# An attention kernel with a soft mixture of experts behind it: two weight tiles loaded into buffers of attention that have gone dead, and the second layer's columns taken in pieces of 128, 256 and 128 with outputs of 256 KB

## The chip, the cores and the metric

The kernel runs on one core of a Trainium2 chip. The metric is device time in microseconds (us), the median of three executions. Five engines work side by side: PE (matrix products, with its own weight loads, PEld), DVE, ACT and POOL (elementwise work and copies), and SP, which here issues nearly all transfers. Sixteen DMA engines move the data between the large memory and the core's buffers.

## The reference

```python
# attention, batch 8, heads 8, sequence 576, head size 64
q_rot, k_rot = rotate(q), rotate(k)                    # rotary embedding
scores = q_rot @ k_rot.T / sqrt(D)
attn = softmax(scores)
x = (attn @ v) -> rows of all heads side by side       # 4608 x 512
# soft mixture of 8 experts with 4 slots each
logits = x @ phi                                       # 4608 x 32
d = softmax over the 4608 rows of logits
slot_input = d.T @ x                                   # 32 slots x 512
for e in range(8):
    h = max(slot_input[e] @ w1[e], 0)                  # 512 -> 1024
    slot_out[e] = h @ w2[e]                            # 1024 -> 512
c = softmax over the 32 slots of logits
out = c @ slot_out                                     # 4608 x 512, float32
```

`w1` and `w2` are 16.8 MB each, the output is 9.4 MB. The slots (32 in all) are so few that the experts are mostly a matter of reading weights.

## The kernel before

**Attention.** 32 pairs of heads (`p` = 0 to 31) go through a fixed list of steps: load and rotate q and k, write them as halves of 16-bit numbers into a tile `hl` (pool `stk`, three buffers of 4,608 bytes a partition, taken in turn), compute row maxima, scores and exponentials, and the products with v (`av`, L363). The order is written out by hand: the tables `WHEN` and `EARLY` give each step a time and the steps are recorded in that order. On PE, ACT and DVE that order is kept to the end of the program; on SP and POOL only up to `steady.close()` (L793), and behind it a scheduler orders POOL's instructions.

**Weights.** The two layers come as 64 tiles of 512 KB (128 partitions of 4 KB), loaded by `load_w` in the order of the list `order`. 28 of them go to the pool `wp` during attention. Near its end `trickle` loads 7 more (pools `wa`, `wx`) where `PACE` says so. The other 29 follow attention, each as soon as a place is free: `wk` and five in `wl` where attention's buffers were (`release_att`), two in `lw` (L800) where the last transposed rows were, two in `wb` (L878) where the normalised rows `xn` were, seven (`N_LEAD`) and then twelve into buffers of `wp` whose first-layer weights have been used by `ffn1` (L892). SP issues all of this from one queue in program order; each transfer also waits for the one eight places ahead of it in the queue.

**Combine weights.** `c_split(q)` (L556) writes the softmax over slots for two batches as a rounded part and a rest into a tile `csp`, the first by ACT, the second by POOL or DVE. `c_tr(q)` transposes it on PE and `c_evac` copies it to `cst` and `crt`. In the kernel before, the tiles `csp0`, `csp1` and two of `cst` are placed in the space of `hl` as soon as the last scores are done (`release_stk`), and `c_split(0)` and `c_split(1)` stand there, with both subtractions on DVE.

**From attention to the experts.** Between L797 and L882 a chain of small steps over PE, DVE, ACT and POOL ends in `slot_t`, the slots' inputs. Two of its links are on POOL: `e_blk` (L857) and `zw` (L859), which PE needs at L863 and L864.

**Experts and output.** `ffn1` has four calls of 16 products of 512 columns (32 in the trace, since each is run in two passes). `ffn2_steps(mh, so)` computes one half of the 512 output columns (256) in 16 steps of four products (eight in the trace), evacuated to `so`. `gather(mh, so)` adds the slots' parts together into `sl`. `combine(mh, sl, b)` makes the output of one batch `b` (or of the rest rows, `b` = 8): two products of 128 columns of `sl` with 512 rows, copied by ACT and by DVE into the halves of one buffer, and one transfer of 512 KB. The two halves are interleaved: `GROUPS` says which combines of the first half stand between how many steps of the second (a negative number is a count of steps).

```python
GROUPS = ((0, 1, -3), (2, 3, -4), (4, 5, 6, -8), (7, "gather", 8))   # L41
```

So PE runs combines 0 and 1, three steps, combines 2 and 3, four steps, 4 to 6, eight steps, then combine 7, the gather of the second half, and combine 8.

Of the kernel before, what the change touches and what calls it, by code (L numbers as in the profile page):

```python
# [19 lines left out]
DM = H * D  # L20
# [10 lines left out]
N_WL = 5  # L31
# [9 lines left out]
GROUPS = ((0, 1, -3), (2, 3, -4), (4, 5, 6, -8), (7, "gather", 8))  # L41
# [13 lines left out]
PACE = {("m_rows", 29): 3, ("m_rows", 30): 3, ("m_rows", 31): 1}  # L55
# [102 lines left out]
def attn_softmoe(ctx, tc, qk, v, phi, w1, w2, cs, ident, sel, seg, out):  # L158
# [5 lines left out]
    wp = ctx.enter_context(tc.tile_pool(name="wp", bufs=N_W))  # L164
    left = ctx.enter_context(ExitStack())
# [5 lines left out]
    early = ctx.enter_context(ExitStack())  # L171
    stk = early.enter_context(tc.tile_pool(name="stk", bufs=N_HL))
# [61 lines left out]
    def high(p, t, c=full):  # L234
        if p not in halves:
            halves[p] = stk.tile([P, 4, S], F16, name="hl")
        nc.scalar.copy(out=halves[p][:, 1 + t, c], in_=loaded[p][:, t, 0, c])  # L237
# [318 lines left out]
    def c_split(q):  # L556
# [3 lines left out]
        (nc.gpsimd if 2 <= q < C_POOL else nc.vector).tensor_tensor(  # L560
# [51 lines left out]
    order.insert(N_W + N_CST + N_WA, swap[-1])  # L612
# [17 lines left out]
    def release_io():  # L630
# [4 lines left out]
        later.extend([(wa, N_CST)] * N_CST + [(wx, N_WA)] * N_WA)  # L635
# [139 lines left out]
    for when, n, q in events:  # L775
# [7 lines left out]
        if (n, q) in scores:  # L783
            scores.remove((n, q))
            if not scores:
# [4 lines left out]
                c_split(1)  # L790
# [5 lines left out]
    next(stat)  # L796
    vals.close()  # L797
# [109 lines left out]
    def ffn2_steps(mh, so):  # L907
        for grp in range(2):
            op = ps_a.tile([P, 512], F32, name="o_ps")
            og = op[:, 0:256]  # L910
            for f in range(8):
                for x in range(4):
                    nc.tensor.matmul(og[32 * x:32 * x + 32, :], lhsT=hts[grp][:, f // 4, f % 4, 32 * x:32 * x + 32],  # L913
                                     rhs=w_tiles[4 * E + 16 * mh + 8 * grp + 4 * (f // 4) + x][:, f % 4, :],
                                     start=(f == 0), stop=(f == 7), tile_position=(0, 32 * x))
                if f == 7:
                    nc.scalar.copy(out=so[:, 0, grp, :], in_=og)
                    nc.vector.tensor_tensor(out=so[:, 1, grp, :], in0=og, in1=so[:, 0, grp, :], op=ALU.subtract)
# [48 lines left out]
    sos = [wp.tile([P, 2, 2, 256], F32R, name="w_exp", bufs=N_W) for _ in range(2)]  # L967
# [10 lines left out]
    steps = ffn2_steps(1, sos[1])  # L978
# [70 lines left out]
```

## Time and profile before

| | us |
|---|---|
| median of 3 runs (492.08 to 494.11) | 492.92 |
| the profiled execution | 490.22 |
| its span, first to last instruction | 488.0 |
| end of attention's last product, from the span's start | 420.9 |
| first-layer products (`ffn1`) begin | 432.3 |
| second-layer products (`ffn2_steps`) begin | 449.1 |
| first output transfer issued | 460.3 |
| the DMA engines fall idle | 486.3 |

| engine | busy us | share of the span |
|---|---|---|
| PE | 458.1 | 94% |
| PEld | 369.2 | 76% |
| DVE | 370.1 | 76% |
| ACT | 298.0 | 61% |
| POOL | 288.0 | 59% |

PE is busy nearly all the time up to 476 us and then not at all, while the DMA engines, half idle during attention, are full from 421 to 486 us. A share over the whole span hides that; the part after attention has to be read by stretches.

### The profile page before, as it was taken

How to read it: one execution, taken by the hardware profiler on the slowest of the kernel's cores; microseconds unless marked ns; L12 is line 12 of the kernel's file. 1: busy time of each engine (PE TensorE's matmuls, PEld its weight loads, DVE VectorE, ACT ScalarE, POOL GpSimd, SP SyncE). 2: the span in 40 equal slices, each digit the busy share in tenths (PEclk: the TensorE clock that was granted, in tenths of full speed). 3: DMA queues.
4: the chain of work that ended last, by engine and by line, in shares of the span. 5: the costliest groups of instructions: out<-in, count | busy, mean ns of one | idle time of the engine just before them, and what ended most of it. 6: DMA issues, size and time to landing. Idle time of an engine off the chain costs nothing.

```text
span 488.0 us, 23673 instructions
## 1 busy us (share of the span) xinstructions
PE 458.1 (94%) x10505; PEld 369.2 (76%) x10505; DVE 370.1 (76%) x624; ACT 298.0 (61%) x681; POOL 288.0 (59%) x318
## 2 busy tenths in 40 slices
PE   4399999999999999999999999999999999999990
PEld 2168788888888888888887888788889888844550
DVE  4979998788879887988898879888977853433271
ACT  2156666775677577657765776567657757463551
POOL 2884869919892879397949694978669102120000
PEclk9689999999999999999999999999999999999996
DMA  7246645563554455435543563254450343499988
GB/s 268 104 184 229 251 136 199 172 222 135 200 170 167 147 195 176 179 126 205 172 174 132 173 205 136 98 167 167 165 189 26 125 160 111 172 375 406 390 352 348
DMA packets 29509, 94.04 MB, mean 193 GB/s; under 512 B 5088, under 2 KB 6880, under 8 KB 29408
## 3 DMA queue, kind: packets, MB, share of 16 engines
q1 hardware_dynamic: 29388, 92.54, 52.2%
q8 instruction: 82, 1.34, 1.1%
q14 instruction: 19, 0.16, 0.1%
q10 hardware_dynamic: 20, 0.00, 0.0%
HBM read 83.02 MB, written 9.44 MB: 189 GB/s over the span
## 4 chain that ended last, share of the span: by engine, by line
PE 87%; DVE 6%; ACT 2%; DMA 2%; issue 1%; SPq 0%; POOL 0%; DVEq 0%; POOLq 0%; ACTq 0%
PE s_ps L363 32%; PE s_ps L328 25%; PE s_ps L275 7%; PE s_ps L343 3%; PE o_ps L913 3%; PE sp_ps L892 3%; PE s_ps L458 2%; DVE nm L277 2%; PE s_ps L717 2%; PE s_ps L437 2%; ACT a_t L329 2%; PE s_ps L284 1%; PE c_ps L939 1%; DVE x_in L232 1%; PE s_ps L520 1%
## 5 line engine op out<-in xcount | busy, mean ns | idle before, releaser
L228 POOL TENSOR_TENSOR x_in<-x_in,cs_sb 128x288 f32<-128x288 f32 x248 | 231.6, 967 | 86.0 <-DMA x_in<-in_qk 77.7
L277 DVE TENSOR_REDUCE nm<-s_ps 128x2 f32<-128x576 f32 x256 | 187.9, 752 | 53.0 <-PE s_ps L275 51.9
L329 ACT ACTIVATE a_t<-s_ps 128x576 f32<-128x576 f32 x256 | 145.7, 659 | 10.3 <-PE s_ps L328 10.2
L363 PEld LDWEIGHTS s_ps<-v_in,a_t 128*64 128x64 f32 x4608 | 138.7, 137 | 11.3 <-ACT a_t L329 3.8
L363 PE MATMUL s_ps<-v_in,a_t 128*64 128x66 f32 x4608 | 144.8, 222 | 0.6 <-ACT a_t L329 0.3
L328 PE MATMUL s_ps<-hl 64*128 64x288 f16 x1536 | 133.8, 283 | 0.3 <-ACT a_t L329 0.2
L328 PEld LDWEIGHTS <-hl 64*128 64x128 f16 x1536 | 79.4, 94 | 19.7 <-issue 9.2
L328 PE MATMUL s_ps<-peak,lift 64*128 64x288 f16 x512 | 75.3, 283 | 0.0
L275 PE MATMUL s_ps<-hl 64*128 64x288 f16 x512 | 66.3, 288 | 6.0 <-DVE nm L277 3.2
L393 ACT COPY o_sb<-s_ps 128x528 f32<-128x528 f32 x31 | 18.6, 600 | 73.6 <-PE s_ps L363 73.6
L411 POOL TENSOR_TENSOR xn<-o_sb,rr 128x640 f32<-128x640 f32 x31 | 43.3, 1404 | 30.8 <-PE s_ps L520 13.9
L237 ACT CAST hl<-x_in 128x576 f16<-128x576 f32 (+1 forms) x66 | 41.0, 657 | 26.0 <-DVE x_in L232 25.9
L241 DVE TENSOR_TENSOR hl<-x_in,hl 128x1152 f16<-128x1152 f32 x32 | 51.7, 1614 | 2.0 <-ACT hl L237 2.0
L232 DVE TENSOR_TENSOR x_in<-x_in 128x1152 f32<-128x1152 f32 (+2 forms) x36 | 50.3, 1399 | 0.1
L275 PEld LDWEIGHTS <-hl 64*128 64x128 f16 x512 | 30.3, 95 | 21.3 <-issue 10.1
L328 PEld LDWEIGHTS <-lift 64*128 64x128 f16 x512 | 27.1, 94 | 4.4
L363 PE MATMUL s_ps<-v_in,a_tr 64*64 64x66 f32 x1152 | 26.1, 224 | 0.0
L363 PEld LDWEIGHTS s_ps<-v_in,a_tr 64*64 64x64 f32 x1152 | 21.6, 133 | 4.9 <-issue 4.2
L286 DVE TENSOR_REDUCE nm<-s_ps 128x2 f32<-128x576 f32 x32 | 23.9, 749 | 1.2 <-PE s_ps L284 0.8
L343 PE MATMUL s_ps<-hl 64*64 64x256 f16 (+1 forms) x384 | 23.5, 287 | 0.1
L347 ACT ACTIVATE a_tr<-s_ps 128x512 f32<-128x512 f32 x32 | 19.1, 597 | 0.8
L447 ACT COPY xt<-s_ps 128x576 f32<-128x576 f32 x31 | 19.0, 656 | 0.0
(168 smaller groups left out, 408.1 us busy)
## 6 DMA issues: line engine op xcount, KB each, us to landing
x_in<-in_qk SPq DMA_DIRECT2D x62, 576.0 KB
w_exp<-in_w SPq DMA_DIRECT2D x63, 512.0 KB
v_in<-in_v SPq DMA_DIRECT2D x32, 330.0 KB
out<-w_exp SPq DMA_DIRECT2D x18, 512.0 KB
peak<-mr SPq DMA_DIRECT2D x126, 0.5 KB
x_in<-in_qk SPq DMA_DIRECT2D x4, 288.0 KB
cs_sb<-in_cs SPq DMA_DIRECT2D x2, 288.0 KB
peak<-mr SPq DMA_DIRECT2D x32, 0.2 KB
```

The lines of the kernel that those rows point to most:

```text
L228: eng.tensor_tensor(out=x[:, :, c], in0=x[:, :, c], in1=cs_sb[:, :, c], op=ALU.mult)
L232: nc.vector.tensor_tensor(out=x[:, t, 0, c], in0=x[:, t, 0, c], in1=x[:, t, 1, c], op=ALU.add)
L237: nc.scalar.copy(out=halves[p][:, 1 + t, c], in_=loaded[p][:, t, 0, c])
L241: nc.vector.tensor_tensor(out=hl[:, 0:4:3], in0=x[:, :, 0], in1=hl[:, 1:3], op=ALU.subtract)
L275: nc.tensor.matmul(s[c, h, 0:HC], lhsT=hl[rows[h], QH, P * j + c.start:P * j + c.stop], rhs=hl[rows[h], KH, half[n]], start=True, stop=True)
L277: nc.vector.tensor_reduce(out=nm[:, n, j:8:4], in_=s[:, :, 0:HC], axis=AX.X, op=ALU.max, negate=True)
L286: nc.vector.tensor_reduce(out=nm[:, :, 8], in_=s[:, :, 0:HC], axis=AX.X, op=ALU.max, negate=True)
L328: nc.tensor.matmul(s[c, h, 0:HC], lhsT=lhs, rhs=rhs, start=(x == 0), stop=(x == 3))
L329: nc.scalar.activation(out=ats[p, b][:, :, half[n]], in_=s[:, :, 0:HC], func=AF.Exp, scale=SCALE)
L343: nc.tensor.matmul(s[rows[h ^ n], n, 0:w] if n else s[rows[h], 0, 512 - w:512], lhsT=lhs, rhs=rhs, start=(x == 0), stop=(x == 3))
L363: nc.tensor.matmul(o[rows[c], h, VW * u:VW * u + VW], lhsT=lhs, rhs=v, start=(i == 0 and u == 0), stop=(left_av[p] == 0 and u == 3 + (c == ...
L411: eng.tensor_tensor(out=xn, in0=t[:, :, :, 0:64], in1=rr.unsqueeze(3).broadcast_to([P, 2, 5, 64]), op=ALU.mult)
```

## The change

1. The pool `stk` stays open to the end. Of its three buffers, two take second-layer weight tiles (`N_WH` = 2), loaded by `trickle` at the end of attention (the `PACE` of the last `m_rows` is 3 instead of 1). These two leave the pool `wl`, which has three places instead of five.
2. The third `hl` buffer takes `csp0` and `crt`. `csp1` and the two `cst` tiles move to attention's released space, so `c_split(1)` moves behind `release_att`, and its subtraction goes to POOL.
3. The second layer's 512 columns are computed in pieces of 128, 256 and 128 (`COLS`) instead of two halves; `w2` is laid out to match. `combine` issues one transfer of 256 KB for each 128 columns, so there are 36 outputs instead of 18; a buffer of 512 KB holds two of them.
4. The interleaving table is used twice: combines of piece 0 among steps of piece 1, combines of piece 1 among steps of piece 2.

```diff
-N_WL = 5
+N_WL = 3
+N_WH = 2
+COLS = ((0, 128), (128, 384), (384, 512))
+W2 = (4 * E, 4 * E + 8, 4 * E + 24)
-GROUPS = ((0, 1, -3), (2, 3, -4), (4, 5, 6, -8), (7, "gather", 8))
+GROUPS = (((0, 1, -3), (2, 3, -4), (4, 5, 6, -8), (7, "gather", 8)), ((0, 1, -3), (2, 3, -4), (4, 5, 6, -8), (7, "gather", 8)))
-PACE = {("m_rows", 29): 3, ("m_rows", 30): 3, ("m_rows", 31): 1}
+PACE = {("m_rows", 29): 3, ("m_rows", 30): 3, ("m_rows", 31): 3}
...
+    stk = ctx.enter_context(tc.tile_pool(name="stk", bufs=N_HL))
     left = ctx.enter_context(ExitStack())
...
-        (nc.gpsimd if 2 <= q < C_POOL else nc.vector).tensor_tensor(
+        (nc.gpsimd if 1 <= q < C_POOL else nc.vector).tensor_tensor(
...
-        if layer == 0:
+        if pool is stk:
+            wt = stk.tile([P, 2 * S], F32, name="hl")[:, 0:1024].rearrange("p (c x) -> p c x", c=4 if layer else 2)
+            pace = None
+        elif layer == 0:
...
-        later.extend([(wa, N_CST)] * N_CST + [(wx, N_WA)] * N_WA)
+        later.extend([(wa, N_CST)] * N_CST + [(wx, N_WA)] * N_WA + [(stk, N_HL)] * N_WH)
...
     def release_stk():
-        early.close()
-        cp = ctx.enter_context(tc.tile_pool(name="cp", bufs=1, side="right", reuse_waits="tile"))
-        csps = [cp.tile([P, 2, 5, 2, NS], F32R, name=f"csp{i}") for i in range(N_CS)]
-        cst = [cp.tile([P, 2, 4, P], F32R, name=f"cst{i}") for i in range(N_CE)]
-        c_tiles.append([cst, None, csps])
+        t = stk.tile([P, 2 * S], F32R, name="hl")
+        first = t[:, 0:640].rearrange("p (b j a n) -> p b j a n", b=2, j=5, a=2)
+        c_tiles.append([[], t[:, 640:2 * S].rearrange("p (b x) -> p b x", b=B), [first]])
...
                 release_stk()
                 c_split(0)
-                c_split(1)
...
     release_att()
     stat = stat_tasks(B - 1)
     next(stat)
+    c_split(1)
     vals.close()
...
-    def combine(mh, sl, b):
-        k = (9 * mh + b) % (N_WA + N_WB)
-        ob = (wb.tile([P, 4, 256], F32, name=f"w_exp{k}") if k < N_WB else
-              extra[0].tile([P, 4, 256], F32, name="w_exp", bufs=N_WA))
-        for jj in range(2):
+    stage = []
+
+    def combine(k, sl, b):
+        first, n = COLS[k][0] // P, (COLS[k][1] - COLS[k][0]) // P
+        for jj in range(n):
+            if not stage:
+                i = next(staged) % (N_WA + N_WB)
+                ob = (wb.tile([P, 2, 512], F32, name=f"w_exp{i}") if i < N_WB else
+                      extra[0].tile([P, 2, 512], F32, name="w_exp", bufs=N_WA))
+                stage.extend((ob[:, 0], ob[:, 1]))
             o = ps_t.tile([P, 512], F32, name="c_ps")
...
-            ob2 = ob.rearrange("p j m -> p (j m)")
-            (nc.vector.tensor_copy if jj else nc.scalar.copy)(out=ob2[:, 512 * jj:512 * jj + 512], in_=o)
-        nc.sync.dma_start(out=out[mh, b], in_=ob2)
+            ob = stage.pop(0)
+            (nc.scalar.copy if len(stage) else nc.vector.tensor_copy)(out=ob, in_=o)
+            nc.sync.dma_start(out=out[first + jj, b], in_=ob)
```

What moves on SP, at the end of attention and behind it (`hl` is a tile of attention that now takes weights, `wk` and `w_exp` are weight tiles, `peak_106` belongs to attention's last pair). Before:

```order
L313 DMA peak_106<-mr 2x2x32
L626 DMA w_exp<-in_w 128x1024
L626 DMA wk<-in_w 128x1024
L626 DMA w_exp<-in_w 128x1024 x5
L660 DMA seg_in<-in_seg 128x320
L626 DMA w_exp<-in_w 128x1024 x2
L626 DMA w_exp_9997<-in_w 128x1024
L626 DMA w_exp_9999<-in_w 128x1024
L626 DMA w_exp<-in_w 128x1024 x19
```

and of the changed kernel:

```order
L315 DMA peak_106<-mr 2x2x32
L631 DMA w_exp<-in_w 128x1024
L631 DMA hl<-in_w 128x1024 x2
L631 DMA wk<-in_w 128x1024
L631 DMA w_exp<-in_w 128x1024 x3
L664 DMA seg_in<-in_seg 128x320
L631 DMA w_exp<-in_w 128x1024 x2
L631 DMA w_exp_9992<-in_w 128x1024
L631 DMA w_exp_9994<-in_w 128x1024
L631 DMA w_exp<-in_w 128x1024 x19
```

Two transfers stand ahead of `wk` and two fewer behind it; the rest of the weights keep their order.

What moves on POOL, between attention and the first layer (`zacc`, `zs`, `zw` are the sums over rows, `e_blk` a factor for the slots, `seg_sb` a table for the gather). Before:

```order
L497 TENSOR_SCALAR zacc<-zacc,al 128x2
L498 TENSOR_TENSOR zacc<-zacc,sd 128x2
L854 TENSOR_SCALAR zs<-zacc 128x1
L855 TENSOR_TENSOR zs<-zs,zacc 128x1
L857 TENSOR_TENSOR e_blk<-id_sb,e_sel 128x128
L859 TENSOR_SCALAR zw<-e_sel,zs 128x32
L560 TENSOR_TENSOR csp_9611<-cn_sb,csp_9611 128x10x32
L661 CAST seg_sb<-seg_in 128x320
L560 TENSOR_TENSOR csp_9612<-cn_sb,csp_9612 128x10x32
```

and of the changed kernel:

```order
L499 TENSOR_SCALAR zacc<-zacc,al 128x2
L500 TENSOR_TENSOR zacc<-zacc,sd 128x2
L858 TENSOR_SCALAR zs<-zacc 128x1
L859 TENSOR_TENSOR zs<-zs,zacc 128x1
L562 TENSOR_TENSOR csp_9836<-cn_sb,csp_9836 128x10x32
L665 CAST seg_sb<-seg_in 128x320
L861 TENSOR_TENSOR e_blk<-id_sb,e_sel 128x128
L863 TENSOR_SCALAR zw<-e_sel,zs 128x32
L562 TENSOR_TENSOR hl<-cn_sb,hl 128x10x32
L562 TENSOR_TENSOR csp_9836<-cn_sb,csp_9836 128x10x32
```

The subtraction of `c_split(1)` and the copy of `seg_sb` now stand ahead of `e_blk` and `zw`.

## Rows read from the trace of the kernel before

**Rows 1.** Page: shares of the last-ending chain by engine; output transfers.
```profile
PE 87%; DVE 6%; ACT 2%; DMA 2%; issue 1%; SPq 0%; POOL 0%; DVEq 0%; POOLq 0%; ACTq 0%
...
out<-w_exp SPq DMA_DIRECT2D x18, 512.0 KB
```

**Rows 2.** Windows: engines' busy us (count), granted clock, DMA share, GB/s.
```profile
411.00:420.00 9.00, 9.00 (x232) 7.80 (x223) 1.88 (x7) 6.65 (x15) 2.94 (x3) 1.00 0.17 58
420.00:421.00 1.00, 1.00 (x48) 0.86 (x44) 0.01 (x1) 0.00 (x0) 0.00 (x0) 1.00 0.00 0
421.00:432.25 11.25, 10.15 (x184) 8.02 (x182) 7.03 (x26) 7.45 (x22) 2.64 (x8) 1.00 0.98 374
432.25:433.50 1.25, 1.25 (x14) 0.42 (x16) 0.00 (x0) 1.22 (x3) 0.99 (x2) 1.00 0.68 259
442.00:460.25 18.25, 18.25 (x228) 9.46 (x224) 3.89 (x10) 7.02 (x15) 0.87 (x1) 1.00 1.02 410
465.00:466.50 1.50, 1.50 (x17) 0.86 (x19) 1.50 (x4) 1.41 (x3) 0.00 (x0) 1.00 0.15 55
466.50:486.25 19.75, 9.87 (x86) 5.73 (x76) 8.67 (x15) 6.73 (x13) 0.00 (x0) 0.82 1.01 399
```

**Rows 3.** Timeline of SP's transfers, short stretches: start, us, line, names, count.
```profile
420.22 0.33 SPq L626 DMA_DIRECT2D wk<-in_w  x1
...
426.06 0.33 SPq L626 DMA_DIRECT2D w_exp<-in_w  x1
...
430.19 0.33 SPq L626 DMA_DIRECT2D w_exp<-in_w  x1
...
434.27 0.33 SPq L626 DMA_DIRECT2D w_exp<-in_w  x1
...
460.28 0.94 SPq L942 DMA_DIRECT2D out<-w_exp  x2
```

**Rows 4.** SP's waits, 427 to 440: us in total, times, longest.
```profile
SPq L626 <- PE sp_ps L380: 3.2, 1, 3.2
...
SPq L626 <- PE sp_ps L892: 5.0, 3, 3.3
```

**Rows 5.** Timeline, 427 to 434, POOL and PE.
```profile
429.47 0.46 POOL L857 TENSOR_TENSOR e_blk<-id_sb,e_sel 128x128 f32<-128x128 f32 x1 [0.35 <-DVE e_sel L856]
429.90 0.39 POOL L859 TENSOR_SCALAR zw<-e_sel,zs 128x32 f32<-128x32 f32 x1
...
430.52 0.31 PE L864 MATMUL t_ps<-zw,bits 128*128 128x32 f32 x2
...
432.51 0.87 POOL L560 TENSOR_TENSOR csp<-cn_sb,csp 128x320 fp32r<-128x320 f32 x1 [2.22 <-ACT csp L559]
...
433.33 0.45 POOL L661 CAST seg_sb<-seg_in 128x320 fp32r<-128x320 f32 x1
```

**Rows 6.** Timeline, 425 to 471, PE, ACT and DVE.
```profile
425.46 0.54 PE L458 MATMUL s_ps<-xt,phi_sb 128*32 128x128 f32 x16 [0.41 <-DVE xt L445]
...
452.51 0.58 ACT L905 COPY wk<-t_ps 128x512 f32<-128x512 f32 x1
...
453.32 3.64 PE L913 MATMUL o_ps<-w_exp,wk 128*32 128x256 f32 x64
...
458.75 1.21 PE L939 MATMUL c_ps<-cst,sl 128*128 128x512 f32 x4
...
469.51 0.73 PE L939 MATMUL c_ps<-w_exp,sl 128*128 128x512 f32 x2
...
470.06 0.42 DVE L918 TENSOR_TENSOR w_exp<-o_ps,w_exp 128x256 fp32r<-128x256 f32 x1 [2.33 <-ACT w_exp L917]
470.40 0.68 DVE L941 COPY w_exp<-c_ps 128x512 f32<-128x512 f32 x1
```

**Rows 7.** DMA queue (packets, MB, share) in 3.5:5.5, then 226.5:227.25, then 477:486.
```profile
q1 hardware_dynamic: 532, 0.58, 96.9%
...
q1 hardware_dynamic: 112, 0.28, 94.0%
...
q1 hardware_dynamic: 1004, 3.65, 102.2%
```

More of the change, by code (lines that the diff above doesn't have):

```diff
@@ L235, in high @@
         if p not in halves:
[L236 removed]
+            halves[p] = stk.tile([P, 4 * S], F16, name="hl").rearrange("p (r s) -> p r s", s=S)
         nc.scalar.copy(out=halves[p][:, 1 + t, c], in_=loaded[p][:, t, 0, c])
@@ L611, in attn_softmoe @@
     order[N_W:N_W] = swap[:-1]
-    order.insert(N_W + N_CST + N_WA, swap[-1])
+    order.insert(N_W + N_CST + N_WA + N_WH, swap[-1])
     def load_w(pool, bufs, tag="w_exp", pace=None):
@@ L650, in release_att @@
         cp = ctx.enter_context(tc.tile_pool(name="cq", bufs=1, side="right", reuse_waits="tile"))
-        c_tiles[0][1] = cp.tile([P, B, 64], F32R, name="crt")
+        c_tiles[0][2].extend(cp.tile([P, 2, 5, 2, NS], F32R, name=f"csp{i}") for i in range(1, N_CS))
+        c_tiles[0][0].extend(cp.tile([P, 2, 4, P], F32R, name=f"cst{i}") for i in range(N_CE))
         seg_in = cp.tile([P, 320], F32, name="seg_in")
@@ L925, in gather @@
                 at = 64 + 128 * grp - 64 * a
-                nc.tensor.matmul(rp[:, 0:256], lhsT=seg_sb[:, at:at + P], rhs=so[:, a, grp, :],
+                nc.tensor.matmul(rp[:, 0:w], lhsT=seg_sb[:, at:at + P], rhs=so[:, a, grp, 0:w],
                                  start=(grp + a == 0), stop=(grp + a == 2))
-        sl = (extra[2].tile([P, 256], F32R, name="kl") if mh else tail.tile([P, 256], F32R, name="sl"))
-        nc.scalar.copy(out=sl, in_=rp[:, 0:256])
-        return sl
-    def combine(mh, sl, b):
-        k = (9 * mh + b) % (N_WA + N_WB)
-        ob = (wb.tile([P, 4, 256], F32, name=f"w_exp{k}") if k < N_WB else
-              extra[0].tile([P, 4, 256], F32, name="w_exp", bufs=N_WA))
-        for jj in range(2):
+        sl = (wp.tile([P, 1024], F32R, name="w_exp", bufs=N_W)[:, 0:w] if w == 256 else
+              tail.tile([P, w], F32R, name=f"sl{k}"))
+        nc.scalar.copy(out=sl, in_=rp[:, 0:w])
+        return sl
+    stage = []
[7 more added lines that the diff above has]
+                stage.extend((ob[:, 0], ob[:, 1]))
             o = ps_t.tile([P, 512], F32, name="c_ps")
@@ L966, in attn_softmoe @@
         c_turns(TURNS[2 * grp + f - 1])
-    sos = [wp.tile([P, 2, 2, 256], F32R, name="w_exp", bufs=N_W) for _ in range(2)]
+    sos = [wp.tile([P, 2, 2, 256], F32R, name="w_exp", bufs=N_W) for _ in COLS]
     steps = ffn2_steps(0, sos[0])
@@ L977, in attn_softmoe @@
             ps_t = ctx.enter_context(tc.tile_pool(name="ps_c", bufs=6, space=PSUM, reuse_waits="tile"))
-    steps = ffn2_steps(1, sos[1])
-    for _ in range(LEAD_STEPS):
-        next(steps)
-    sl0 = gather(0, sos[0])
-    c_tr(turned)
-    late_evac = c_evac_late(turned)
-    for run_of in GROUPS:
-        for b in run_of:
-            if isinstance(b, str):
-                sl1 = gather(1, sos[1])
-            elif b < 0:
-                for _ in range(-b):
-                    next(steps, None)
-            else:
-                combine(0, sl0, b)
-                if b:
-                    next(late_evac, None)
+    late_evac = None
+    sls = []
+    for k, groups in enumerate(GROUPS):
+        steps = ffn2_steps(k + 1, sos[k + 1])
+        for _ in range(LEAD_STEPS):
+            next(steps)
+        if not sls:
+            sls.append(gather(0, sos[0]))
+            c_tr(turned)
+            late_evac = c_evac_late(turned)
+        for run_of in groups:
+            for b in run_of:
+                if isinstance(b, str):
+                    sls.append(gather(k + 1, sos[k + 1]))
+                elif b < 0:
+                    for _ in range(-b):
+                        next(steps, None)
+                else:
+                    combine(k, sls[k], b)
+                    if b:
+                        next(late_evac, None)
     for b in range(B + 1):
-        combine(1, sl1, b)
+        combine(len(GROUPS), sls[-1], b)
 def kernel(q, k, v, moe_phi, moe_w1, moe_w2):
```

30 lines of the change are left out of this document (18 added, 12 removed).

## The prediction

> **What bounds the kernel now.** I read the chain of waits first. PE has 87% of it and DMA 2% [rows 1]; that is the attention part, which this change leaves alone except for three small operations near its end. So the question is only the 67 us behind attention's last product, and there I read the windows by stretch. From 421 us the DMA engines are full: 374 GB/s up to 432.25, 410 GB/s from 442 to 460.25, and again a share of 1.01 from 466.5 to 486.25, when the last output has gone and PE has long been idle. Two stretches stand out: a dip to 0.68 at 432.25 to 433.5, and a hole at 465 to 466.5 with a share of 0.15 [rows 2]. Hence the end is set by the transfers, and by the moments at which they have nothing to move. The time of the end is "the last hole closes, plus what is left to write".
>
> Then SP's timeline and waits, to see what transfers wait for. The issue of `wk` at 420.22 is followed by data only after 421.0 [rows 2, 3], so a transfer issued into an empty queue shows its data about 0.9 us later. The two `lw` follow at 426.06, the two `wb` at 430.19, the first of the seven lead tiles at 434.27 [rows 3]. The waits before the last two are on PE: 3.2 us, and 5.0 us of which one is 3.3 [rows 4]. These loads are late because the buffers are in use until then, not because the DMA engines are behind. That is the point of the whole case.
>
> **Part 1: two tiles loaded early.** At 410 GB/s [rows 2] a tile of 524 KB costs 1.28 us, so 2.56 us leave the stretch behind attention. The room for them is there: between 411 and 420 the DMA share is 0.17 [rows 2], and the transfers of the two queue ahead of `wk` on SP, which is not issued before 420.22 anyway. So their own cost is nothing.
>
> But what becomes of the 2.56 us? In the kernel before, `wk`, five `wl`, `seg_in` (0.16 MB) and two `lw` are 4.36 MB, which at 374 GB/s from 421.0 last to about 432.7; there the dip lies. The two `wb` then carry on to about 435.8, and the first lead tile, available from 434.27 + 0.9 = 435.2, follows without a hole. In the changed kernel four tiles and `seg_in` are 2.26 MB, done at 427.1; the `lw` are available at 427.0 and done at 429.9; the `wb` are available at 431.1 (a hole of 1.2) and done at 433.8; the first lead tile is available at 435.2 at best. The lead tiles therefore begin between 435.2 and 435.9, against 435.8 before: of 2.56 us saved, 0 to 0.6 us arrives, and part 2 takes that. The 19 tiles from there on are the same. I keep the end of the weights where it is, near 460.6.
>
> **Part 2: POOL's new order.** The subtraction of `c_split(1)` (0.87 us, by the row of L560) and the copy of `seg_sb` (0.45 us) now stand ahead of `e_blk` and `zw` on POOL [rows 5]. POOL is free at about 429.1, so `e_blk` (0.46 us) starts at about 430.4 instead of 429.47 and `zw` (0.39 us) ends at about 431.2 instead of 430.3 [rows 5]. PE's L864 needs `zw` and stood at 430.52 [rows 5]. Everything on PE behind it, `ffn1` and the release of the lead tiles' buffers with it, moves by about 0.7 us (from 0, if PE's own work hides it, to 1.3, the two operations in full). `seg_in` is itself behind four tiles instead of six, so its data are there before POOL asks. The subtraction that DVE no longer does was off the path and gives nothing back.
>
> **Part 3: pieces of 128, 256 and 128.** PE's 256-column products take 3.64/64 = 0.057 us each in the trace. With 128 columns they should take half, 0.0285; the row of L458, half of them 128 columns wide and half 64, has 0.54/16 = 0.034 with the same weight loads [rows 6]. I take 0.030. The first piece has 128 of these, so 128 x 0.027 = 3.4 us are saved before the first gather. One cover is lost: the last 32 of them need the copy of L905 by ACT, which ends at 453.1 [rows 6], after the shift at 453.8. PE gets there at about 453.4 and waits 0.4 us. With the 0.7 us of part 2 and two or three tenths of rounding between them, the first gather comes 2.0 us earlier. Outputs then start while the last weights still come in, and stand behind them in the queue; that gains nothing by itself.
>
> What counts is the hole. Between weights and the second gather the changed kernel has 9 outputs of 256 KB to write, not 9 of 512 KB, while PE still runs all 256 columns of piece 1 among them. Combines 0 to 6 now have 7 products instead of 14, at 1.21/4 = 0.30 us [rows 6], so 2.1 us less, and the gather is 0.2 us shorter. Combine 7 stood at 469.51 [rows 6]; it now starts at 469.5 - 2.0 - 2.1 - 0.2 = 465.2. Its copy stands on DVE behind the evacuation of piece 1 (L918, 0.42 us) and ended at 470.40 + 0.68 = 471.1, 1.6 us behind its start [rows 6]. So output 7 is ready at 466.8 and its data flow at 467.7. Outputs 0 to 6, 1.8 MB, are through by 460.6 + 3.5 x 1.32 = 465.2. The hole is 2.5 us long and ends 1.2 us later than the one before, which ended at 466.5 [rows 2].
>
> Behind it the writes run without a hole, as they did before: copies make an output every 0.35 us on two engines, and the queue needs about 0.66. The buffers hold 14 outputs. Before, 15 of the 18 outputs [rows 1] went from 466.5 to 486.25, 1.317 us for 512 KB [rows 2]. Now 29 of 256 KB remain, 19.1 us instead of 19.75; combine 8 comes 0.1 us late.
>
> **Rows of 2 KB.** An output row is now 2,048 bytes per partition instead of 4,096. No transfer of before has this size. In the queue's rows, 4,096-byte packets cost 1.022 x 16 x 9 us / 891 = 165 ns (3.65 MB are 891 of them), 2,640-byte ones 0.94 x 16 x 0.75 / 106 = 106 ns, 1,152-byte ones 0.969 x 16 x 2 / 503 = 62 ns [rows 7]. The line through the upper two puts 2,048 bytes at 83 ns, two for 165, no loss; the line from 1,152 to 4,096 puts it at 93, so 21 ns are lost on each pair. An engine has 8 pairs for 512 KB and one more completion. Over 14.5 pairs of outputs that is 0 to 2.4 us. I take 0.8, nearer to the 2,640-byte row, which is the nearest in size.
>
> The Trainium skill, "DMA: Bandwidth & Descriptors", section "Why small descriptors are slow (HBM only)", gives about 3 cycles of overhead per packet over one cycle for each 32 bytes. By that two packets of 2,048 bytes are 134 cycles against 131, an estimate of 2.3% or 0.4 us in the sum; these rows, with 1,152 bytes at 62 ns, ask for more than that.
>
> **The sum**, against the profiled execution (490.22, span 488.0; the median of the runs is 492.92, and I add the same difference to it): hole closes later +1.2, combine 8 +0.1, fewer bytes left -0.65, small rows +0.8: +1.45 us. That is 491.7 for the execution and **494.4 us** for the median. 0.5% of it, 2.5 us, is about what a measurement of this kernel can tell from no change.
>
> **Rivals.**
> - *Bytes decide* (faster). If the holes vanish and the two tiles count in full, the weights end at 458.0 and 18 x 1.317 + 0.9 = 24.6 us of output follow: the DMA ends at 482.6, 3.6 us earlier, 489.3 us. For it: the share of 1.02 from 442 on [rows 2]. Against it: both loads before that wait for PE [rows 4], and output 7 hangs on PE, not on weights.
> - *Only the hole vanishes.* The combine path is 2.5 us faster than I think, the weights end at 460.6: 485.2, 1.0 us earlier, 491.9 us.
> - *Small rows cost what the 1,152-byte line says* (slower): 2.4 instead of 0.8, +3.05 us, 496.0 us. It decides from about 90 ns per 2,048-byte packet on, where the sum passes 2.5 us.
> - *Fixed cost per transfer shows.* Each of 18 more transfers exposes the 0.9 us between issue and data: +16 us, 510 us. Eight may be in flight, and 512 KB follow each other without a dip [rows 2], which speaks against it. The Trainium skill, "DMA: Bandwidth & Descriptors", section "Bandwidth", says to batch transfers to 1 MiB or more; by that rule halving the outputs is the wrong direction, but the trace shows the fixed part hidden.
>
> **Chances.** Forecast 0.64 (its own range 492.6 to 496.2, of which 0.12 lies over +0.5%), bytes decide 0.09, only the hole vanishes 0.10, small rows 0.15, fixed cost 0.02. So faster 0.09, same 0.52 + 0.10 = 0.62, slower 0.12 + 0.15 + 0.02 = 0.29. The range from 491.0 to 496.8 leaves out the two ends.
>
> **What would show it.** Right: a DMA share near zero twice between 430 and 435.5; `e_blk` near 430.4 and `ffn1` near 433.0; the first output issued near 457; a hole before about 467.7 longer than 1.5 us; 0.68 us per 256 KB behind it. Wrong: weights ending before 459, which makes the loads bound by bytes; `ffn1` still at 432.3, which makes POOL's order harmless; combine 7 before 463.5, which closes the hole; packets of outputs above 90 ns, which makes it slower than forecast.

## The result, and the profile after

The changed kernel takes 495.49 us (median of 20 runs, 493.08 to 502.86) against 492.90 for the kernel before in the same rounds: ratio 1.0053, interval 1.0032 to 1.0074. That is 2.6 us slower, 1.1 more than forecast: a small difference, but the whole interval lies above 1. Ratios, here and below, leave out runs over 1.5% longer than the fastest of their kernel; of the profiles only that of after_short_middle is of such a run (499.05 us, with 6 us more in attention than after). The profiled execution took 493.69 us (span 492.0), 3.47 more than that of before.

First the page: the chain's shares, the queue, the transfers.

```profile
PE 82%; DVE 7%; DMA 3%; ACT 3%; issue 2%; POOL 0%; SPq 0%; DVEq 0%; ACTq 0%; POOLq 0%
...
q1 hardware_dynamic: 31980, 92.54, 52.5%
...
out<-w_exp SPq DMA_DIRECT2D x36, 256.0 KB
```

It answers to [rows 1]: 36 outputs of half the size. The chain tells little else, since most of it is attention.

Attention itself ended later here: its last product, in the kernel before and then in the one after (timeline of PE: start, us, line, names).

```profile
420.07 0.81 PE L363 MATMUL s_ps<-v_in,a_tr 64*64 64x66 f32 x36
```

```profile
421.56 0.81 PE L365 MATMUL s_ps<-v_in,a_tr 64*64 64x66 f32 x36
```

That is 1.49 us, nearly half of the difference between the two executions, in a part that the change hardly touches. So a place behind attention is given below as its distance from the end of that product, "at +45" and so on; 420.88 is the zero of before, 422.37 of after (422.36 in the table below, which adds unrounded records).

Windows of the kernel after (engines' busy us with counts, granted clock, DMA share, GB/s), for [rows 2]:

```profile
421.00:432.25 11.25, 9.67 (x224) 7.46 (x220) 6.27 (x22) 6.22 (x20) 3.33 (x9) 1.00 0.78 291
432.25:433.50 1.25, 1.06 (x9) 1.00 (x9) 0.76 (x5) 1.23 (x3) 0.50 (x2) 1.00 0.53 151
433.50:442.00 8.50, 8.50 (x78) 3.26 (x78) 1.37 (x4) 3.38 (x8) 0.87 (x1) 1.00 0.78 288
442.00:457.00 15.00, 14.53 (x225) 7.67 (x223) 4.00 (x11) 6.50 (x15) 0.87 (x1) 1.00 1.02 408
...
468.00:469.50 1.50, 1.43 (x13) 0.81 (x13) 0.73 (x2) 0.86 (x2) 0.00 (x0) 1.00 0.09 33
470.00:489.75 19.75, 10.91 (x149) 7.47 (x147) 9.06 (x16) 7.70 (x16) 0.00 (x0) 0.89 1.01 377
```

Three things are to be seen. Up to 442 us the queue idles much more than before: 0.78 where it was 0.98. From 442 it is full again, as before. And behind a hole at 468.0 to 469.5 the outputs run with a share of 1.01 but at 377 GB/s, where before had 399: the same engines, just as busy, move less.

The idle stretches are in SP's timeline:

```profile
419.59 0.33 SPq L631 DMA_DIRECT2D wk<-in_w  x1
420.02 2.70 SPq L631 DMA_DIRECT2D w_exp<-in_w  x3
422.78 0.43 SPq L664 DMA_DIRECT2D seg_in<-in_seg  x1
427.70 27.18 SPq L631 DMA_DIRECT2D w_exp<-in_w  x23
460.90 8.94 SPq L955 DMA_DIRECT2D out<-w_exp  x9
```

Between `seg_in` at 422.78 and the first `lw` at 427.70 nothing is issued. The `lw` stand at +5.3, in before at +5.2 [rows 3]: fewer transfers stand ahead of them, but their own release did not come sooner.

POOL, and PE's weight load that waits for it (for [rows 5]):

```profile
430.70 0.87 POOL L562 TENSOR_TENSOR csp<-cn_sb,csp 128x320 fp32r<-128x320 f32 x1
431.53 0.44 POOL L665 CAST seg_sb<-seg_in 128x320 fp32r<-128x320 f32 x1
431.94 0.45 POOL L861 TENSOR_TENSOR e_blk<-id_sb,e_sel 128x128 f32<-128x128 f32 x1
432.37 0.37 POOL L863 TENSOR_SCALAR zw<-e_sel,zs 128x32 f32<-128x32 f32 x1
...
432.44 0.30 PEld L867 LDWEIGHTS o_ps<-e_blk,acc 128*128 128x128 f32 x2 [0.57 <-POOL e_blk L861]
```

`e_blk` starts at +9.57; it stood at +8.59. PE now waits 0.57 us for it, and the product with `zw` starts at +10.4 instead of +9.65.

And the second layer (PE, ACT and DVE), for [rows 6]:

```profile
456.96 0.68 PE L933 MATMUL c_ps<-w_exp,seg_sb 128*128 128x128 f32 x4
458.08 0.71 PE L952 MATMUL c_ps<-cst,sl 128*128 128x512 f32 x2
...
460.29 0.59 ACT L954 COPY w_exp<-c_ps 128x512 f32<-128x512 f32 x1 [2.34 <-PE o_ps L920]
...
463.58 3.66 PE L920 MATMUL o_ps<-w_exp,wk 128*32 128x256 f32 x64
467.17 0.50 PE L952 MATMUL c_ps<-w_exp,sl 128*128 128x512 f32 x1
...
467.71 0.42 DVE L924 TENSOR_TENSOR w_exp<-o_ps,w_exp 128x256 fp32r<-128x256 f32 x1 [2.98 <-ACT w_exp L923]
468.05 0.68 DVE L954 COPY w_exp<-c_ps 128x512 f32<-128x512 f32 x1
```

The first gather is at 456.96, at +34.6 where it was at +36.4; combine 7 at 467.17, behind 64 products (as the trace counts them) of the 256-column piece, and its copy only at 468.05. That copy ends the hole. The ACT row was not expected: the first two combines are done at 458.8, but their copies start at 460.29, when the second piece's first steps are done.

### The profile page after: what moved, and what is told of

The parts are those of the page before. It is cut to its first block, busy times and chain, and to the rows that moved or that the text cites. A ratio compares the mean times of both kernels' runs of the same rounds, so it can differ in the third digit from the quotient of the medians.

```text
span 492.0 us, 23999 instructions
## 1 busy us (share of the span) xinstructions
PE 459.0 (93%) x10637; PEld 371.4 (75%) x10637; DVE 371.4 (75%) x625; ACT 298.4 (61%) x684; POOL 287.0 (58%) x319
## 4 chain that ended last, share of the span: by engine, by line
PE 82%; DVE 7%; DMA 3%; ACT 3%; issue 2%; POOL 0%; SPq 0%; DVEq 0%; ACTq 0%; POOLq 0%
PE s_ps L365 30%; PE s_ps L330 24%; PE s_ps L277 7%; PE s_ps L345 4%; PE sp_ps L896 3%; DVE nm L279 3%; PE o_ps L920 3%; PE s_ps L460 2%; PE s_ps L439 2%; DVE hl L243 2%; DVE x_in L234 2%; PE s_ps L286 1%; DMA v_in<-in_v 1%; PE c_ps L952 1%; PE s_ps L522 1%
## 5 line engine op out<-in xcount | busy, mean ns | idle before, releaser
L330 PEld LDWEIGHTS <-hl 64*128 64x128 f16 x1536 | 78.8, 94 | 19.8 <-issue 9.0
L413 POOL TENSOR_TENSOR xn<-o_sb,rr 128x640 f32<-128x640 f32 x31 | 42.2, 1370 | 31.2 <-PE s_ps L522 14.0
L243 DVE TENSOR_TENSOR hl<-x_in,hl 128x1152 f16<-128x1152 f32 x32 | 54.1, 1690 | 2.0 <-ACT hl L239 2.0
L234 DVE TENSOR_TENSOR x_in<-x_in 128x1152 f32<-128x1152 f32 (+2 forms) x36 | 48.6, 1352 | 0.1
L277 PEld LDWEIGHTS <-hl 64*128 64x128 f16 x512 | 29.7, 95 | 22.1 <-issue 10.3
L345 PE MATMUL s_ps<-hl 64*64 64x320 f16 (+1 forms) x384 | 23.1, 287 | 1.4 <-issue 0.7
(176 smaller groups left out, 420.9 us busy)
```

The source lines that it names most:

```text
L234: nc.vector.tensor_tensor(out=x[:, t, 0, c], in0=x[:, t, 0, c], in1=x[:, t, 1, c], op=ALU.add)
L243: nc.vector.tensor_tensor(out=hl[:, 0:4:3], in0=x[:, :, 0], in1=hl[:, 1:3], op=ALU.subtract)
L277: nc.tensor.matmul(s[c, h, 0:HC], lhsT=hl[rows[h], QH, P * j + c.start:P * j + c.stop], rhs=hl[rows[h], KH, half[n]], start=True, stop=True)
L330: nc.tensor.matmul(s[c, h, 0:HC], lhsT=lhs, rhs=rhs, start=(x == 0), stop=(x == 3))
L345: nc.tensor.matmul(s[rows[h ^ n], n, 0:w] if n else s[rows[h], 0, 512 - w:512], lhsT=lhs, rhs=rhs, start=(x == 0), stop=(x == 3))
L413: eng.tensor_tensor(out=xn, in0=t[:, :, :, 0:64], in1=rr.unsqueeze(3).broadcast_to([P, 2, 5, 64]), op=ALU.mult)
```

## The experiments

Attention's end varies between executions by far more than the effects looked for, so each profile is read by one more number: the stretch from the end of attention's last product to the end of the last output packet, both from the records of the trace. (The first two expectations below give it as 65.4 and 67.4, read from the ends of windows; by the packets' records it is 65.63 and 68.07.)

```
kernel                attention's end  last byte  stretch   ratio to before [interval]
before                     420.88       486.51     65.63
before_again               425.54       491.25     65.71
after                      422.36       490.43     68.07    1.0053 [1.0032, 1.0074]
after_again                422.59       490.60     68.01    1.0044 [1.0021, 1.0067]
before_small_outs          422.34       489.54     67.20    1.0030 [0.9997, 1.0063]
after_tiles_late           426.83       495.03     68.20    1.0051 [1.0025, 1.0077]
after_pool_order           423.05       491.08     68.03    1.0041 [1.0010, 1.0073]
after_two_tiles_less       425.85       493.97     68.12    1.0041 [1.0008, 1.0073]
after_short_middle         428.52       495.82     67.30    1.0017 [0.9979, 1.0055]
after_pairs                422.53       491.06     68.52    1.0050 [1.0017, 1.0083]
after_pool_held            423.09       490.23     67.14    1.0036 [1.0008, 1.0064]
four_pieces                422.51       495.70     73.19    1.0114 [1.0084, 1.0145]
four_pieces_pairs          424.04       497.76     73.72    1.0129 [1.0092, 1.0166]
four_pieces_ring           424.04       490.38     66.34    0.9996 [0.9968, 1.0023]
```

**Both kernels again.** Nothing is edited.

> The kernel before, unchanged, once more. In the two profiles at hand attention's last product ended at 420.9 us of the span before and at 422.4 after, 1.5 us that no step of the prediction holds. Theory (variation between executions): attention's end moves by some tenths to 1.5 us between profiles of one and the same kernel, and the stretch from that end to the last output byte (65.4 us before, 67.4 after) stays within 0.3 us. Rival (the change itself slows attention, by the new place of the tiles or the two loads inside it): before shows 420.9 again within 0.3, and after 422.4.

> The changed kernel, unchanged, once more, beside the one above. Theory (variation): attention's end falls anywhere between 420.5 and 422.5, the stretch from there to the last output byte is again 67.4 within 0.3, and the ratio to before is 1.003 to 1.006. Rival (attention is slower by the change): attention ends at 422.4 again within 0.3, 1.5 us behind that of the kernel before, and the ratio is above 1.005.

The kernel before, in a second execution:

```profile
424.73 0.81 PE L363 MATMUL s_ps<-v_in,a_tr 64*64 64x66 f32 x36
```

Its attention ended 4.66 us later than in the first, three times what was expected at most and later than in either profile of the changed kernel, and its one time was 494.98 us. The stretch behind it was 65.71, within 0.1. After again: attention's end at 422.59, near the 422.36 of the first, the stretch 68.01, within 0.1 of 68.07, and the ratio 1.0044, under the 1.005 that the rival asked for. So the 1.5 us inside attention say nothing on the change, and the change costs 2.4 us behind attention, which is what the medians show (2.6). The rival is out.

**Small outputs alone**, in the kernel before:

```diff
-        nc.sync.dma_start(out=out[mh, b], in_=ob2)
+            nc.sync.dma_start(out=out[2 * mh + jj, b], in_=ob2[:, 512 * jj:512 * jj + 512])
...
```

> The kernel before with nothing but its outputs sent in halves: 36 transfers of 256 KB in rows of 2 KB instead of 18 of 512 KB in rows of 4 KB. Theory (a row of 2 KB takes 87 ns in after where half a row of 4 KB takes 82): the outputs behind the hole, 0.686 us per 256 KB before, take 0.70 each, so the end is 0.4 to 1.2 us later and the time 493.2 to 494.0, ratio 1.001 to 1.002. Rival A (a fixed cost for each transfer, some 0.5 us): 36 x 0.5 = 18 us later, about 510. Rival B (rows cost as at the 1152-byte line of the profile, 3 us over the whole): 496, ratio 1.006, which would be the whole loss of the change.

The stretch is 67.20, 1.5 us longer: more than the 0.4 to 1.2 expected, half of rival B's 3, nowhere near rival A. The rate is told best by 16 us in which nothing but outputs moves, +48.5 to +64.5: before, then this kernel, then the changed one.

```profile
469.38:485.38 16.00, 6.99 (x30) 4.16 (x26) 7.45 (x12) 6.73 (x13) 0.00 (x0) 0.81 1.01 402
```

```profile
470.84:486.84 16.00, 6.92 (x30) 4.16 (x26) 7.46 (x12) 6.72 (x13) 0.00 (x0) 0.81 1.03 382
```

```profile
470.86:486.86 16.00, 10.05 (x133) 6.88 (x123) 8.20 (x15) 6.84 (x15) 0.00 (x0) 0.95 1.02 378
```

PE, ACT and DVE do the same in the first two, so the fall from 402 to 382 GB/s comes with the small outputs: a row of 2 KB takes more than half the time of one of 4 KB (worked out below). At 402 a tile of 256 KB takes 0.652 us, at 378 0.694: over the 29 tiles behind the hole, 1.2 us.

**Two tiles late**, with their loads written behind attention, into the same buffers:

```diff
-    order.insert(N_W + N_CST + N_WA + N_WH, swap[-1])
+    order.insert(N_W + N_CST + N_WA, swap[-1])
...
-        later.extend([(wa, N_CST)] * N_CST + [(wx, N_WA)] * N_WA + [(stk, N_HL)] * N_WH)
+        later.extend([(wa, N_CST)] * N_CST + [(wx, N_WA)] * N_WA)
...
             load_w(wl, N_WL)
+        for _ in range(N_WH):
+            load_w(stk, N_HL)
```

> The changed kernel with its two early weight tiles loaded behind attention again, into the same two buffers, where the kernel before loads them. Theory (later loads wait for buffers that other work releases, so the two early tiles only leave the queue idle sooner): the idle stretches between 427 and 437.5 us shrink, the weights end within 0.5 us of where they end in after, the end does not move: ratio to before as for the changed kernel within 0.001. Rival (bytes decide): the two tiles, 1.05 MB at 400 GB/s, cost 2.6 us again, the last output lands 2.6 us later, about 498.

68.20 against 68.04 (the mean of the two of after). But SP's timeline shows that the two loads did not move behind attention, which ends at 426.83 here:

```profile
416.28 0.55 SPq L631 DMA_DIRECT2D hl<-in_w  x1
...
421.64 0.33 SPq L631 DMA_DIRECT2D hl<-in_w  x1
424.07 0.33 SPq L631 DMA_DIRECT2D wk<-in_w  x1
```

They still stand ahead of `wk`, the one 10.6 us before attention's end as in after, the other 5.2. Behind `steady.close()` the order on SP is the scheduler's too, not that of the source. So this run says nothing on what the early loads are worth. The issue times of the other runs do. These are the issues of the first lead tile in after, then in after_pool_held (below), which has the early loads too but POOL's old order:

```profile
436.65 0.33 SPq L631 DMA_DIRECT2D w_exp<-in_w  x1
```

```profile
436.49 0.33 SPq L637 DMA_DIRECT2D w_exp<-in_w  x1
```

That is +14.3 and +13.4; before, with two tiles more ahead of it, had +13.4 as well [rows 3]. The early loads let the loads behind them be issued no sooner, as the prediction had it.

**Two tiles less:**

```diff
-            while len(w_tiles) < 8 * E:
+            while len(w_tiles) < 8 * E - 2:
                 load_w(wp, N_W)
+            w_tiles[8 * E - 2] = w_tiles[8 * E - 1] = w_tiles[8 * E - 3]
```

> The changed kernel without the loads of its last two weight tiles (1.05 MB); two tiles of the same shape stand in for them in the products, so half of the second group's part of the last piece is computed with other weights. Theory (the last product of the middle piece decides when the hole closes, not the bytes): the weights end 2.6 us sooner, the hole opens that much sooner and closes where it did, the end stays within 0.4 us: about 495.4. Rival (bytes decide): the end comes 2.6 us sooner, about 492.9.

68.12, against 68.04: the last weight row landed 3.0 us sooner (+38.9 instead of +41.9), and the end does not come sooner. This puts *bytes decide* out.

**A shorter middle piece:**

```diff
-                for x in range(4):
+                for x in range(4 if k != 1 or f < 6 else 0):
...
-                                     rhs=wt[:, w * c:w * c + w], start=(f == 0), stop=(f == 7), tile_position=(0, 32 * x))
+                                     rhs=wt[:, w * c:w * c + w], start=(f == 0), stop=(f == (5 if k == 1 else 7)), tile_position=(0, 32 * x))
```

> The changed kernel without 4 of the 16 steps of the middle piece of the second layer (the last quarter of each group's contraction is left out in columns 128 to 383). Theory (the hole closes when PE has done the middle piece): 4 steps of 0.54 us less, the outputs behind the hole start 1.5 us sooner (the hole is 1.5 us long), the end comes 1.5 us sooner: about 494.0, and the queue has no hole left. Rival (bytes decide, or the staging buffers): the end does not move by more than 0.3 us.

67.30, 0.74 us sooner: half of what was expected. Combine 7 came 1.25 us sooner (+43.4 instead of +44.6), but a hole of 1.0 us remained, now at +42.5, ahead of the fourth output instead of the eighth. In that kernel too the first combine's copies start when the second piece's first steps are done (four_pieces below tells why), and the fourth output is issued only at +41.6. SP took 1.40 us for that issue, where those ahead of the hole in after took 0.33 to 0.70:

```profile
470.11 1.40 SPq L955 DMA_DIRECT2D out<-w_exp  x1
```

So PE's middle piece does set the hole of after, as the theory says. What left the second hole, the late copies or that long issue, was not tried, and why the issue took so long is open. Behind attention, up to +45, the granted clock is 1.00 here as in after.

**GpSimd's order**, in two attempts. The first moved the two lines in the source:

```diff
...
     nc.gpsimd.tensor_scalar_mul(out=zw, in0=e, scalar1=zs)
+    c_rest(1)
+    nc.gpsimd.tensor_copy(out=c_tiles[1][0], in_=c_tiles[1][1])
...
```

> The changed kernel with the GpSimd work between attention and the first layer in the order of the kernel before: the second slot block's subtraction (0.87 us) and the copy of seg (0.44 us) behind e_blk and zw, not ahead of them. Theory: e_blk and zw are done 0.7 us sooner measured from attention's end, the first layer, the release of the lead buffers and the second layer follow, the hole in the output closes 0.7 us sooner, and the time is 0.7 us less than after: about 494.8, ratio to before 1.004. Rival (PE waits for something else there by then, or the queue has slack behind it): nothing moves by more than 0.2 us at the end.

The stretch is 68.03, unchanged. But POOL's timeline shows the old order:

```profile
431.25 0.86 POOL L568 TENSOR_TENSOR csp<-cn_sb,csp 128x320 fp32r<-128x320 f32 x1
432.06 0.44 POOL L870 CAST seg_sb<-seg_in 128x320 fp32r<-128x320 f32 x1
432.48 0.45 POOL L866 TENSOR_TENSOR e_blk<-id_sb,e_sel 128x128 f32<-128x128 f32 x1
```

The scheduler put first what was ready first, wherever it was written. The run tested nothing. The second ties the two behind `zw`:

```diff
...
-    nc.gpsimd.tensor_scalar_mul(out=zw, in0=e, scalar1=zs)
+    zw_of = nc.gpsimd.tensor_scalar_mul(out=zw, in0=e, scalar1=zs)
+    with tc.issue_after(zw_of.ins):
+        c_rest(1)
+        nc.gpsimd.tensor_copy(out=c_tiles[1][0], in_=c_tiles[1][1])
...
```

> The run after_pool_order moved two lines in the source, but its trace shows GpSimd doing them ahead of e_blk all the same: the scheduler puts first what is ready first, so that run says nothing on the step. Here the subtraction and the copy of seg are tied behind zw on GpSimd's queue. Measured from the end of attention's last product (attention's own end moves by up to 7.6 us between executions of one kernel), after and its repeats start the zw product at 10.29 to 10.44 us, before at 9.65, and the last output byte lands at 68.0 to 68.1, before at 65.6 to 65.7. Theory: the zw product starts at 9.65 again, the second layer 0.7 us sooner (28.3), the hole in the output closes 0.6 sooner and the last byte lands at 67.4: about 494.8. Rival (the subtraction behind zw makes the second block's transposes late, which PE then waits for): the product starts at 9.65 but the second layer still at 29.0, and the end does not move.

```profile
431.68 0.46 POOL L866 TENSOR_TENSOR e_blk<-id_sb,e_sel 128x128 f32<-128x128 f32 x1 [0.35 <-DVE e_sel L865]
432.13 0.38 POOL L868 TENSOR_SCALAR zw<-e_sel,zs 128x32 f32<-128x32 f32 x1
432.48 0.86 POOL L568 TENSOR_TENSOR csp<-cn_sb,csp 128x320 fp32r<-128x320 f32 x1
```

With zero at 423.09, `e_blk` is at +8.59 as in before. The `zw` product starts at +9.65, the second layer at +28.25 (+28.98 in after_again), combine 7 at +43.9 (+44.6), and the last byte lands at 67.14, 0.9 us sooner than in after. Two operations on an engine that is 58% busy cost nearly 1 us at the end, 58 us later.

**Pairs**: the changed kernel, two neighbouring tiles in one transfer.

```diff
...
-            nc.sync.dma_start(out=out[first + jj, b], in_=ob)
...
+            sent.append((first + jj, b))
+            if h:
+                nc.sync.dma_start(out=out[len(sent) // 2 - 1], in_=stage.pop(0).rearrange("p h x -> p (h x)"))
...
```

> The changed kernel with two neighbouring output tiles sent as one transfer of 512 KB in rows of 4 KB, as the kernel before sends them. Theory (rows of 2 KB cost 5 ns a row more than half a row of 4 KB, 87 against 82): behind the hole 27 tiles take 0.686 instead of 0.698 us, 0.3 us, and the last transfer starts some 0.4 us later: nearly the same, 495.0 to 495.5. Rival (the small rows are most of the loss): the end comes 1.2 us or more sooner, under 494.3.

68.52, 0.5 us later. The rows are cheaper again (390 GB/s in the same 16 us, 0.5 us of which is a new hole), but the seventh tile now has to wait for its partner, the eighth: the hole starts at +44.9 instead of +45.7, one tile more is left behind it, and a second one opens at +48.5. Large transfers and a close supply pull against each other where one hole decides.

**Four pieces** of 128 columns, on after_pool_held, with single tiles and with pairs:

```diff
-COLS = ((0, 128), (128, 384), (384, 512))
+COLS = ((0, 128), (128, 256), (256, 384), (384, 512))
-W2 = (4 * E, 4 * E + 8, 4 * E + 24)
+W2 = (4 * E, 4 * E + 8, 4 * E + 16, 4 * E + 24)
...
+GROUPS = (((0, 1, -3), (2, 3, -4), (4, 5, 6, -8), (7, "gather", 8)),) * 3
```

> after_pool_held with the second layer's columns in four pieces of 128. Theory (the hole is there because nine output tiles of the first piece have to cover a middle piece of 256 columns, whose last quarter, left out, moved the end 0.7 us): with pieces of 128 the second piece is summed up some 4 us sooner, the outputs have no hole (1.9 us of idle queue between 35 and 50 us behind attention goes), and the last byte lands at 65.6 to 66.0 behind attention's end, level with before: about 493. Rival (PE, which has 12 more steps' overhead and the same products, cannot keep up with 0.7 us a tile): new holes behind the second and third piece, and the end is at 67.4 or later.

> The kernel of four_pieces with neighbouring output tiles sent in pairs of 512 KB in rows of 4 KB. Theory (rows of 2 KB cost 1.3 us over some 29 tiles: 373 GB/s against 399 in the stretch behind the hole): with no hole left that pairs could make longer, the last byte lands 0.9 to 1.3 us sooner than in four_pieces, at 64.5 to 65.0 behind attention's end, sooner than before's 65.6: about 492, ratio 0.998. Rival (as in after_pairs, where a pair waits for its second tile and the end came 0.5 us later): 66.0 or later.

Both were far worse, 73.19 and 73.72, and for a reason that neither text gives. Four_pieces, ACT and DVE, then windows:

```profile
460.58 0.58 ACT L962 COPY w_exp<-c_ps 128x512 f32<-128x512 f32 x1 [3.37 <-PE o_ps L928]
460.58 0.69 DVE L962 COPY w_exp<-c_ps 128x512 f32<-128x512 f32 x1 [4.06 <-PE o_ps L928]
...
463.48 3.61 PE L928 MATMUL o_ps<-w_exp,wk 128*32 128x128 f32 x64
```

```profile
460.00:464.00 4.00, 2.20 (x35) 1.24 (x31) 2.72 (x7) 2.35 (x7) 0.00 (x0) 0.94 0.85 329
464.00:468.00 4.00, 3.60 (x62) 2.82 (x54) 0.79 (x2) 0.89 (x3) 0.00 (x0) 0.63 0.03 10
```

The combines' copies wait for products of the second piece. The ring of staging tiles begins at the two `wb` tiles, and these hold weights that the second piece reads: in after the one in its steps 1 to 4 and the other in 5 to 8, in four_pieces the one in steps 1 to 8 and the other in 9 to 16. The copies wait for those steps, and PE's next combines for the copies. PE is busy 2.20 of 4 us, and in the next 4 us its granted clock is 0.63, a mean between its two levels of 1.2 and 2.4 GHz, while the queue stands still (10 GB/s). The last run begins the ring at the five tiles that are free by then:

```diff
-                i = next(staged) % (N_WA + N_WB)
+                i = (next(staged) + N_WB) % (N_WA + N_WB)
```

> The kernel of four_pieces_pairs with its ring of staging tiles begun at the five tiles that hold first-layer and first-piece weights, not at the two that hold weights of the second piece. Why: in four_pieces the copies of the first two combines, done on TensorE 3.0 us before, start only when four more steps of the second piece are done, and the third and fourth wait for the step after that, since the two first staging tiles hold weights that those steps read; TensorE then waits, its granted clock falls to 0.63, and the output stands still for 5 us. Theory: without that wait TensorE does a 16-step piece in 3.6 us and nine combines in 3.2, as fast as nine output tiles land (6.2), the first output is issued at 37.6 behind attention's end, there is no hole over 0.5 us from then on, and with rows of 4 KB the last byte lands at 64.3 to 65.0, against 65.6 to 65.7 before and 67.1 in after_pool_held: ratio to before 0.997 to 1.000. Rival (four pieces keep TensorE, ACT and DVE too busy for the output's rate, whatever the staging): holes behind the second and third piece as in four_pieces (52 to 55, 58 and 64 us behind attention's end), and the last byte at 67 or later.

66.34: by this one line 7.4 us sooner than four_pieces_pairs, so the staging was the cause there. The same 64 products:

```profile
462.86 1.95 PE L928 MATMUL o_ps<-w_exp,wk 128*32 128x128 f32 x64
```

They take 1.95 us at the full clock, 3.61 in four_pieces. But 64.3 to 65.0 was expected. Windows of this kernel:

```profile
470.00:474.00 4.00, 4.00 (x82) 2.82 (x80) 2.01 (x5) 1.71 (x4) 0.00 (x0) 1.00 0.95 375
474.00:478.00 4.00, 4.00 (x67) 2.48 (x63) 2.22 (x5) 1.73 (x4) 0.00 (x0) 1.00 0.81 317
478.00:482.00 4.00, 3.93 (x74) 3.13 (x74) 1.58 (x4) 1.90 (x5) 0.00 (x0) 1.00 0.66 262
```

PE is busy throughout and the queue is not: the rival holds in a milder form, PE has become the bound of these 12 us. Behind them the queue is full again (share 0.96 from 482 to 486 us) and PE nearly done. The time is level with before (0.9996, interval 0.9968 to 1.0023), the stretch still 0.6 to 0.7 us longer. None of these versions beats it.

## Why the prediction was right, and where it was short

The mechanism was right and the sum was short: +1.45 us forecast, 2.4 behind attention and 2.6 in the medians.

- *Part 1, early tiles worth nothing: right.* The idle time forecast between 430 and 435.5 is there, the lead tiles are issued no sooner than before, and the run with two tiles less moved the end by 0.08 us, where 2.6 was the rival's price. The forecast kept the end of the weights where it was and read it as 460.6, +39.7. It did stay, but stands later: counted by the bytes that the queue moved, all weights were through at +40.4 to +40.6 in both executions of both kernels. In after_pool_held, without the delay of part 2, it was +40.1: within the 0 to 0.6 us of gain that the forecast allowed.
- *Part 2, POOL's order, 0.7 us: right.* `e_blk` was forecast at 430.4 and stands at 430.5 on the time scale of before (+9.57 and 420.88); the `zw` product is 0.6 to 0.8 late, and undoing it gives back 0.9 at the end.
- *Part 3, the hole: right in what ends it, 0.3 us short in when, wrong in when it opens.* Combine 7 was forecast at 465.2 and stands at 465.7 (+44.8; 465.5 in after_again); the hole ends at +47.1 to +47.2 against +45.6, so 1.5 to 1.6 us later where 1.2 was forecast. It is 1.5 us long, not 2.5, because it opened 1.3 us later, at +45.6 where 465.2 is +44.3. Of this, 0.7 to 0.9 is the later end of the weights. Most of the rest is a dip in the queue between the first outputs:

```profile
463.50:464.00 0.50, 0.50 (x9) 0.29 (x12) 0.50 (x2) 0.50 (x3) 0.00 (x0) 1.00 0.60 229
464.00:464.50 0.50, 0.50 (x17) 0.29 (x12) 0.50 (x2) 0.50 (x2) 0.00 (x0) 1.00 0.68 250
```

  Their copies were held by the staging tiles: the first output was issued at +38.5 (459.4) instead of about 457, the third at +41.0. That wait was missed. It did not hold up combine 7, as PE was busy without a break from 460 to 468 us, and the sum, which counts from the hole's end, does not have it; in four_pieces_pairs it cost 7.4 us.
- *Small rows, 0.8 us: the term that was mis-sized.* It is 1.2. From the queue's share in after over 477 to 486 us:

```profile
q1 hardware_dynamic: 1891, 3.45, 102.7%
```

  3.45 MB are 1,685 rows of 2,048 bytes, so a row, with its part of the transfer's completion, takes 1.027 x 16 x 9 us / 1,685 = 88 ns; half of the 165 for 4,096 bytes is 82.5 [rows 7]. The line through the upper two sizes had given 83, that through 1,152 bytes 93; the truth lies between them, where the sum had leaned to the upper. 29 tiles are 232 rows on each of 16 engines: 232 x 5.2 ns = 1.2 us. By the rule of the Trainium skill that the prediction cites ("DMA: Bandwidth & Descriptors", section "Why small descriptors are slow (HBM only)"), it would be 0.4, an estimate; the trace, with 1.2, does not agree.
- *The sum again:* hole 1.5 to 1.6 instead of 1.2, one tile of 256 KB less behind it -0.65 as forecast, rows 1.2 instead of 0.8, and 0.3 that is not resolved further, at the stream's two ends, where 0.1 for combine 8 was forecast: 2.4. Both large terms were too small, so no error hid another.
- *Rivals.* Fixed cost per transfer would have shown as 18 us in before_small_outs, which lost 1.5. That loss counts all 36 tiles and a hole that closed later with fewer tiles behind it; how much of it is rows alone was not separated, only the rate was. Not tried: the ring begun at free tiles in the changed kernel itself, and its effect on the hole of after_short_middle.

## What to carry to other kernels

When a stream of transfers waits for buffers, moving loads ahead of it only lengthens the wait; look for what releases the buffers, and for the work put ahead of that on an engine that seems idle. Where a scheduler orders an engine's work, read in the trace whether an edit moved what it was to move: two of the runs here did not. Before new columns, tiles or pieces are laid out, ask for each staging buffer which instruction reads its old content last, since a finer split can turn a free ring into a stall. Where executions differ by several us in a long, untouched part, measure from a landmark behind it: here this told effects of 0.2 us apart, where the intervals of the ratios are 1 us wide to either side at best.

## What the runs showed of the hardware

- Attention's last product ended between 420.9 and 428.5 us in these profiles, 420.9 and 425.5 for one and the same kernel, while the 65 to 68 us behind it repeated within 0.1 for the two kernels profiled twice. What sets attention's length was not looked into.
- POOL's work held DVE up. In after the multiplication that makes `e_sel` takes

```profile
430.83 0.79 DVE L860 TENSOR_TENSOR e_sel<-e_sel,sel_sb 128x32 f32<-128x32 f32 x1 [0.29 <-ACT e_sel L838]
```

  and in after_pool_held, where POOL's subtraction does not run beside it,

```profile
431.41 0.19 DVE L865 TENSOR_TENSOR e_sel<-e_sel,sel_sb 128x32 f32<-128x32 f32 x1 [0.29 <-ACT e_sel L843]
```

  In after it ends at 431.62, as POOL's subtraction does (430.70 + 0.87, within 0.05). The subtraction itself takes 0.86 to 0.87 us in all these traces. The Trainium skill, "SBUF — State Buffer", section "Who interferes with whom", says that a DVE instruction with two inputs in SBUF contends with a GpSimd instruction that reads SBUF; the trace agrees. It cost nothing more here, as `e_blk` waited for POOL anyway.
- Products of 128 columns take 0.030 us each at the full clock (1.95 us for 64), those of 256 columns 0.057 (3.66 for 64): nearly half, as the prediction's 0.030 had it.
